# The opening of an adaLN block: c loaded as four rows and turned by one transpose, silu moved ahead, four more unread products

## The chip, the cores and the metric

The kernel runs on one core of a Trainium2 chip. The metric is device time in microseconds (us) of one execution. A core has five engines that run side by side, each through its own instructions in order: TensorE (PE in the profile; its weight loads are PEld), VectorE (DVE), ScalarE (ACT), GpSimd (POOL) and SyncE (SP). SP and ACT also issue transfers (DMAs) between device memory and the on-chip memory; each has a queue for them.

## The reference, cut to what matters

```python
x = A_x                                                   # 1 x 2048 x 512
mod = (_silu(c) @ w_mod).reshape(1, 6, 1, 512)            # c: 1 x 512, w_mod: 512 x 3072
sa, ca, ga, sb, cb, gb = (mod[:, i] for i in range(6))
h = _layernorm(x) * (1 + ca) + sa
x = x + ga * linear_attention(h, A_wqkv, A_wo)            # 32 heads of 16, phi = elu + 1
h = _layernorm(x) * (1 + cb) + sb
x = x + gb * (((h @ B_w_gate) * (h @ B_w_up)) @ B_w_down) # inner width 1376
```

Everything is float32. The first thing that attention needs is h: the normalized rows of x, scaled by 1 + ca and shifted by sa. These two vectors come from c and from columns of w_mod. So the opening of the kernel has two strands that meet: the statistics of the first 512 rows of x, and silu(c) times two column blocks of w_mod.

## The kernel before, in words

**Tiling.** The 2048 rows of x are worked in four chunks of four tiles, 128 rows each. A float32 product is made of three products of rounded halves (high by high, high by low, low by high), so a projection of 128 rows by 512 columns over a depth of 512 is 12 products of 128 x 128 by 128 x 512. The stages follow each other: K, V and Q work with the first normalization; the attention's output; the gated part with its second normalization, as a block product with sums of halves; the product with w_down. The order of the instructions on each engine is the order in which the code calls them: nothing is rescheduled. Most on-chip buffers come from one pool of 99 tiles, and products go to two pools of four PSUM banks.

**The opening** is written out by hand at lines 457 to 538. Its parts, by function and line:

- Transfers (127 to 143): the four x tiles of the first chunk go by turns to SP's and ACT's queue. Then SP takes c as one row of 512 (line 130). Then come halves of two column blocks of w_mod (`load_half`: 256 columns of two k), two on each queue, and the rest on SP. Line 56 says which rows of w_mod a partition holds: `(p k)`, so partition p holds rows 4p to 4p + 3. Transfers are counted by eight completion counters in turn; a transfer waits until the one eight before it, which used the same counter, has landed.
- `keep_on(n)` (152 to 154) issues n products of zeros into a bank that nobody reads.
- `silu_a` (163 to 167) turns c from one row into four columns: a product of each 128-element piece with a single one. ACT then takes exp(-c). `silu_b` (169 to 172) makes silu from it with three small steps on VectorE, into `sc`.
- `Norm.stats` (253, 254), `rstd_of` (262 on VectorE, 265 on POOL) and `nmr_of` (270) give mean and deviation of two tiles at a time. `xhat` (280 on ACT, 277 on VectorE) writes a normalized tile, and `transpose_token` (294) turns its four 128 x 128 pieces on TensorE.
- The scale and shift: `block_pe` (403) multiplies pieces of w_mod with `sc` on TensorE, depth by depth. `half_sum` (179 on ACT, 183 on VectorE) instead sums four scaled rows of w_mod per partition into a tile f; `block_one` (414) then adds f over the partitions with a product by ones. `block_out` (418) writes 128 values of each vector into `both`.
- `mod_h` (425), `mod_f` (432) and `mod_l` (437) apply scale and shift and split the result in halves. `weight_h` (442) and `weight_l` (445) split the weights. `cells` (454) are the products of the first projection (K).

The order on TensorE is thus: 14 unread products; c turned; 1 unread; tile 0 transposed; 2 unread; tile 1 transposed; the scale or shift by `block_pe` of the first 128 columns; 1 unread; tiles 3 and 2 transposed; `block_one`; 2 unread; the sums of the next 128 columns; `cells`.

Of the kernel before, what the change touches and what calls it, by code (L numbers as in the profile page):

```python
# [14 lines left out]
P = 128  # L15
# [7 lines left out]
def tile_adaln_block(  # L23
# [12 lines left out]
    nc = tc.nc  # L36
# [3 lines left out]
    KD = D // P  # L40
    NJ = 4
# [8 lines left out]
    xv = x[0].rearrange("(c p j) d -> c j p d", p=P, j=NJ)  # L50
# [2 lines left out]
    wo_v = wo.rearrange("(k p) n -> k p n", p=P)  # L53
    wg_v = w_gate.rearrange("(k p) f -> p k f", p=P)
    wu_v = w_up.rearrange("(k p) f -> p k f", p=P)
    wm_v = w_mod.rearrange("(p k) n -> p k n", k=KD)

    pool = lambda name, bufs, **kw: ctx.enter_context(tc.tile_pool(name=name, bufs=bufs, **kw))
    consts = pool("consts", 1)
# [10 lines left out]
    def T(p, tag, shape=(P, D), dt=F32, bufs=None):  # L70
        cnt[0] += 1
        return p.tile(list(shape), dt, tag="t" if p is tiles else tag, name=f"{tag}_{cnt[0]}", bufs=bufs)

    def B(tag, shape=(P, D), dt=F32):

        return T(tiles, tag, shape, dt)
# [8 lines left out]
    ident = consts.tile([P, P], F32, name="ident")  # L85
    make_identity(nc, ident)
    ones = consts.tile([P, 1], F32, name="ones")
# [21 lines left out]
    def load(src, tag, by=None):  # L109
        raw = B(tag, (P, *src.shape[1:]))[:src.shape[0]]  # L110
        (by or nc.sync).dma_start(raw, src)
        return raw
# [12 lines left out]
        return [load(wqkv_v[k, :, n * D:(n + 1) * D], "raw") for k in range(KD)]  # L125

    two = (nc.sync, nc.scalar)
    xts = [[load(xv[0, j], "x", two[j % 2]) for j in range(NJ)]]
    c_row = B("f")[:1]
    nc.sync.dma_start(c_row, c)  # L130
    raw_half = {}
    raw_half[1, 0] = load_half(1, 0, two)
    raw_half[0, 0] = load_half(0, 0, two)
# [18 lines left out]
    def keep_on(n):  # L152
        for _ in range(n):
            nc.tensor.matmul(ps_idle, idle[:, :P], idle, start=True, stop=True)  # L154
# [6 lines left out]
    ct = ps_m[:, 4 * KD:5 * KD]  # L161

    def silu_a():
        of_k = c_row.rearrange("o (p k) -> o k p", k=KD)
        for k in range(KD):
            nc.tensor.matmul(ct[:, k:k + 1], of_k[:, k], ones[:1], start=True, stop=True)
        nc.scalar.activation(ce, ct, AF.Exp, scale=-1.0)

    def silu_b():
        nc.vector.tensor_scalar(ce, ce, 1.0, None, op0=ALU.add)  # L170
        nc.vector.reciprocal(ce, ce)
        nc.vector.tensor_mul(sc, ct, ce)
# [212 lines left out]
    n0 = norm[0]  # L385
# [21 lines left out]
    def half_sum(v, half, *ks, on=None):  # L407
        if 0 in ks:
            sums[v, half] = B("f")[:, :D // 2]
        mod_acc(sums[v, half], [raw_half[v, half][k // 2][:, k % 2] for k in range(KD)], ks, on)  # L410
# [29 lines left out]
    def weight_h(k):  # L440
        wk.append((B("w", dt=F32R), B("w", dt=F32R)))
        nc.scalar.activation(wk[k][0], raw_k[k], AF.Copy)
# [11 lines left out]
                nc.tensor.matmul(kps[t], x[:, t * P:(t + 1) * P], w, start=k == 0 and part == 0,  # L454
                                 stop=k == KD - 1 and part == 2)

    keep_on(14)
    n0.stats(0)
    nc.vector.tensor_copy(ones_r, ones.to_broadcast([P, P]))
    n0.stats(1)  # L460
    n0.rstd_of(0, 2)
    n0.stats(2)
    n0.nmr_of(0, 2)
    n0.xhat(0)
    silu_a()
    keep_on(1)
    n0.xhat(1)
    n0.stats(3)
    n0.rstd_of(2, 4)
    n0.transpose_token(0)  # L470
    silu_b()
    half_sum(0, 0, 0, on=nc.scalar)
    n0.nmr_of(2, 4)
    n0.xhat(2)
# [3 lines left out]
    block_pe(1, 0)  # L478
    half_sum(0, 0, 1, 2, 3)
    weight_h(0)  # L480
    keep_on(1)
    n0.transpose_token(3)
    n0.transpose_token(2)
    block_one(0, 0)
# [151 lines left out]
    for i in range(4, NT):  # L636
        ch, j = divmod(i, NJ)
# [910 lines left out]
```

## Time and profile before

| | us |
|---|---|
| median of three timed runs | 561.05 (560.29, 561.05, 563.6) |
| the profiled execution's own time | 556.42 |
| its span, first to last instruction | 554.5 |
| TensorE busy in the span | 547.8 |
| VectorE, ScalarE, GpSimd busy | 420.2, 297.1, 176.9 |

The profile is of one execution. Times in its rows count from the start of the span. A row of the chain of waits has start, length and what ran, followed back from the last instruction; a row of the timeline has start, length, engine, line, operation and tiles (written <- read), shape and count, and in brackets the idle time ahead of it with what ended it; a row of a window table gives, for a stretch, its length, and for each engine its busy time and how many instructions began, then the granted clock of TensorE, the busy share of the transfer engines and the rate in GB/s. Lines of the tables refer to the kernel before.

### The profile page before, as it was taken

Reading aid. Unit: us, or ns where it says so; the run is one execution under the profiler, and the core shown is the slowest. Engines: PE = TensorE matmul, PEld = TensorE weight load, DVE = VectorE, ACT = ScalarE, POOL = GpSimd, SP = SyncE. Lnnn points to the kernel's source line nnn. Section 1 sums busy time; section 2 is a strip of 40 time slices with the busy share of each in tenths; the row PEclk is TensorE's granted clock in tenths of the full one; section 3 lists DMA queues with packets and bytes.
Section 4 is the critical chain, followed back from the end, with each engine's and each line's share of the span. In section 5 each row is a group of like instructions: output and inputs, shape, how many; then the busy total and the mean of one; then the engine's idle time right before and its main releaser. Section 6 shows DMA issues by size and latency. Waiting matters only on the chain.

```text
span 554.5 us, 8037 instructions
## 1 busy us (share of the span) xinstructions
PE 547.8 (99%) x2744; PEld 460.8 (83%) x2744; DVE 420.2 (76%) x755; ACT 297.1 (54%) x528; POOL 176.9 (32%) x183
## 2 busy tenths in 40 slices
PE   8999999999999999999999999999999999999996
PEld 7888888888888888888888888878888888888886
DVE  5868779978998998865655766854567878778696
ACT  4976858456567876654545355442443525443540
POOL 2000000003527645343556644400512524242400
PEclk9999999999999999999999999999999999999999
DMA  8900224203230045195888635499575534442004
GB/s 287 386 11 1 76 77 151 77 1 76 77 115 2 0 155 186 39 316 178 284 285 276 218 123 202 157 373 331 177 262 190 182 122 147 133 139 77 0 1 152
DMA packets 56746, 83.75 MB, mean 151 GB/s; under 512 B 6593, under 2 KB 21697, under 8 KB 56706
## 3 DMA queue, kind: packets, MB, share of 16 engines
q1 hardware_dynamic: 55874, 82.21, 44.2%
q10 hardware_dynamic: 832, 1.05, 0.5%
q8 instruction: 21, 0.34, 0.3%
q14 instruction: 19, 0.16, 0.1%
HBM read 53.54 MB, written 29.69 MB: 150 GB/s over the span
## 4 chain that ended last, share of the span: by engine, by line
PE 99%; DVE 0%; issue 0%; DVEq 0%
PE bank L1039 38%; PE acc L1198 8%; PE acc L853 8%; PE bank L222 5%; PE bank L224 5%; PE bank L223 5%; PE acc L1121 4%; PE acc L1122 4%; PE acc L1123 4%; PE acc L373 3%; PE acc L372 3%; PE acc L371 3%; PE bank L287 2%; PE acc L454 2%; PE acc L154 1%; PE bank L828 1%
## 5 line engine op out<-in xcount | busy, mean ns | idle before, releaser
L1039 PE MATMUL bank<-h,w 128*128 128x512 f32 (+1 forms) x924 | 220.5, 391 | 0.0
L1039 PEld LDWEIGHTS bank<-h,w 128*128 128x128 f32 (+1 forms) x924 | 168.7, 186 | 36.6 <-issue 0.4
L1045 ACT ACTIVATE bank<-bank 128x512 f32<-128x512 f32 (+1 forms) x45 | 26.2, 581 | 131.0 <-PE bank L1039 130.7
L1002 POOL TENSOR_TENSOR w<-raw,w 128x256 fp32r<-128x256 f32 (+3 forms) x22 | 24.2, 1100 | 79.7 <-ACT w L995 64.9
L1222 DVE TENSOR_TENSOR x<-acc,x 128x256 f32<-128x256 f32 x108 | 39.2, 415 | 10.2 <-PE acc L1198 9.6
L1198 PE MATMUL acc<-w,kh 128*128 128x256 f32 x252 | 46.8, 282 | 0.0
L222 PE MATMUL bank<-w,h 128*128 128x512 f32 x112 | 44.1, 394 | 0.0
L1198 PEld LDWEIGHTS acc<-w,kh 128*128 128x128 f32 x252 | 41.4, 190 | 3.1 <-DVE x L1222 0.2
L224 PE MATMUL bank<-w,h 128*128 128x512 f32 x112 | 43.7, 390 | 0.0
L223 PE MATMUL bank<-w,h 128*128 128x512 f32 x112 | 43.7, 390 | 0.0
L853 PE MATMUL acc<-w,xh 128*128 128x512 f32 x128 | 40.7, 399 | 0.0
L1065 DVE TENSOR_TENSOR phi<-bank,g 128x512 f32<-128x512 f32 (+1 forms) x22 | 15.1, 687 | 29.8 <-PE bank L1039 28.4
L702 POOL TENSOR_TENSOR f<-h,zb 128x512 f32<-128x512 f32 x12 | 17.5, 1472 | 62.9 <-ACT zb L682 48.8
L265 POOL TENSOR_TENSOR rstd<-ve,half 128x4 f32<-128x4 f32 (+3 forms) x12 | 10.5, 879 | 82.9 <-DVE ve L262 70.5
L1095 DVE TENSOR_TENSOR g<-bank,u 128x512 f32<-128x512 f32 (+1 forms) x22 | 15.2, 690 | 28.4 <-ACT u L1045 25.0
L1121 PE MATMUL acc<-w,kh 128*128 128x512 f32 (+1 forms) x92 | 35.9, 390 | 0.0
L1122 PE MATMUL acc<-w,kh 128*128 128x512 f32 (+1 forms) x92 | 35.9, 390 | 0.0
L1123 PE MATMUL acc<-w,kl 128*128 128x512 f32 (+1 forms) x92 | 35.8, 389 | 0.0
L1198 PE MATMUL acc<-w,kl 128*128 128x256 f32 x126 | 35.6, 283 | 0.0
L1045 ACT ACTIVATE u<-bank 128x512 f32<-128x512 f32 (+1 forms) x44 | 26.2, 595 | 12.6 <-PE bank L1039 12.4
L1128 DVE TENSOR_TENSOR x<-acc,x 128x512 f32<-128x512 f32 x44 | 28.1, 681 | 5.8 <-PE acc L1123 5.8
L280 ACT ACTIVATE n<-x,nmr,rstd 128x512 f32<-128x512 f32 x31 | 23.7, 807 | 11.2 <-DVE nmr L270 11.0
(198 smaller groups left out, 1189.1 us busy)
## 6 DMA issues: line engine op xcount, KB each, us to landing
right<-w SPq DMA_DIRECT2D x56, 256.0 KB, 3.8
w<-right SPq DMA_DIRECT2D x56, 256.0 KB, 3.6
x<-in_A_x_dram SPq DMA_DIRECT2D x22, 256.0 KB, 5.4
raw<-in_w_mod_dram SPq DMA_DIRECT2D x22, 256.0 KB, 3.5
raw<-in_B_w_down_dram SPq DMA_DIRECT2D x20, 256.0 KB, 3.2
side_s<-h SPq DMA_DIRECT2D x16, 256.0 KB, 2.6
h<-side_s SPq DMA_DIRECT2D x16, 256.0 KB, 5.7
raw<-in_A_wqkv_dram SPq DMA_DIRECT2D x12, 256.0 KB, 5.4
```

Of the source, the lines that this page charges most:

```text
L222: nc.tensor.matmul(ps, ah, bh, start=begin and i == 0, stop=False)
L223: nc.tensor.matmul(ps, ah, bl, start=False, stop=False)
L224: nc.tensor.matmul(ps, al, bh, start=False, stop=end and i == n - 1)
L853: nc.tensor.matmul(yps[i], x, y, start=fresh and k + n == 0, stop=k == KD - 1 and n == 2, skip_group_check=True)
L1039: mm = lambda x, y, **kw: nc.tensor.matmul(ps, x[:, k], y, skip_group_check=True, **kw)
L1045: nc.scalar.activation(out, x, AF.Copy)
L1121: nc.tensor.matmul(dn[j], hh[:n, a:b], dh[:n], start=i == 0, stop=False)
L1122: nc.tensor.matmul(dn[j], hh[:n, a:b], dl[:n], start=False, stop=False)
L1123: nc.tensor.matmul(dn[j], hl[:n, a:b], dh[:n], start=False, stop=i == n_of - 1)
L1128: nc.vector.tensor_tensor(xt, dn[j], xt, op=ALU.add)
L1198: mm = lambda x, y, **kw: nc.tensor.matmul(ps, x[:, a:b], y, skip_group_check=True, **kw)
L1222: nc.vector.tensor_tensor(xt[:, halves[at]], banks[b][:, part], xt[:, halves[at]], op=ALU.add)
```

## The change

The c vector is loaded as four rows of 128, second on ACT's queue between its two x tiles, and one transpose with a 4 x 4 identity turns it into 128 x 4. Since element 128k + p of c now stands in partition p, column k, w_mod is viewed in the same order, `(k p)`, wherever it is loaded. The turn and the exponential (`silu_a`) move ahead of the normalization, behind 13 unread products, with 5 behind them. `silu_b` moves ahead of the statistics of the fourth tile. The normalization of tiles 0 and 1 on ACT is issued together. One more unread product stands behind the sums of `half_sum`, ahead of the transposes of tiles 3 and 2. That is three more unread products around the turn (18 instead of 15) and one more later.

```diff
-    wm_v = w_mod.rearrange("(p k) n -> p k n", k=KD)
+    wm_v = w_mod.rearrange("(k p) n -> p k n", p=P)
...
-    xts = [[load(xv[0, j], "x", two[j % 2]) for j in range(NJ)]]
-    c_row = B("f")[:1]
-    nc.sync.dma_start(c_row, c)
+    xts = [[load(xv[0, j], "x", two[j]) for j in range(2)]]
+    c_k = B("f")[:KD, :P]
+    nc.scalar.dma_start(c_k, c[0].rearrange("(k p) -> k p", p=P))
+    xts[0] += [load(xv[0, 2 + j], "x", two[j]) for j in range(2)]
...
     def silu_a():
-        of_k = c_row.rearrange("o (p k) -> o k p", k=KD)
-        for k in range(KD):
-            nc.tensor.matmul(ct[:, k:k + 1], of_k[:, k], ones[:1], start=True, stop=True)
+        nc.tensor.transpose(ct, c_k, ident[:KD, :KD])
         nc.scalar.activation(ce, ct, AF.Exp, scale=-1.0)
...
-    keep_on(14)
+    keep_on(13)
+    silu_a()
+    keep_on(5)
     n0.stats(0)
...
     n0.nmr_of(0, 2)
-    n0.xhat(0)
-    silu_a()
-    keep_on(1)
-    n0.xhat(1)
+    n0.xhat(0, 1)
+    silu_b()
     n0.stats(3)
     n0.rstd_of(2, 4)
     n0.transpose_token(0)
-    silu_b()
     half_sum(0, 0, 0, on=nc.scalar)
...
     weight_h(0)
-    keep_on(1)
+    keep_on(2)
     n0.transpose_token(3)
```

## The prediction, made before the changed kernel was run

> **What bounds the kernel now.** I read the page first: the span, the busy shares, the granted clock and the chain that ended last.
>
> ```profile
> span 554.5 us, 8037 instructions
> ...
> PE 547.8 (99%) x2744; PEld 460.8 (83%) x2744; DVE 420.2 (76%) x755; ACT 297.1 (54%) x528; POOL 176.9 (32%) x183
> ...
> PEclk9999999999999999999999999999999999999999
> ...
> PE 99%; DVE 0%; issue 0%; DVEq 0%
> ```
>
> TensorE is busy for 547.8 of 554.5 us and carries 99% of the chain, at a granted clock in its top tenth in every slice. So time is saved only by taking work off TensorE, or by starting its useful work earlier; whatever moves the first projection moves the end by the same amount, as long as TensorE then runs on without holes.
>
> The diff touches only the opening, so I went next to the chain of waits of the first 16 us. A row gives start, length, line and count of TensorE's work; L154 is the unread product, L166 the four products that turn c, L294 the transposes of normalized rows, L403 and L414 the scale and shift sums, L454 the first projection of K.
>
> ```profile
> 1.98 5.17 PE acc L154 x14
> 7.15 1.95 PE acc L166 x8
> 9.11 0.43 PE acc L154
> 9.53 0.44 PE bank L294 x4
> 9.97 0.47 PE acc L154 x2
> 10.43 0.44 PE bank L294 x4
> 10.87 0.79 PE acc L403 x8
> 11.66 0.34 PE acc L154
> 12.00 0.87 PE bank L294 x8
> 12.87 0.12 PE acc L414 x2
> 12.99 0.57 PE acc L154 x2
> 13.56 0.79 PE acc L403 x8
> 14.34 0.22 PE acc L414 x2
> 14.56 1.26 PE acc L454 x5
> ```
>
> TensorE has no hole here, but part of this is filling: twenty unread products in all, eight half-passes for c (1.95 us), and only from 14.56 on useful products. To see what really gates that point I took the timeline of the same stretch. (A row: start, length, engine, line, what is written from what; in brackets idle time before it and what ended it.)
>
> ```profile
> 5.07 1.28 ACT L280 ACT_TABLE_LOAD   x1 [5.07 <-DMA x<-in_A_x_dram]
> ...
> 6.85 0.71 POOL L265 TENSOR_TENSOR rstd<-ve,half 128x2 f32<-128x2 f32 x1 [4.13 <-DVE ve L262]
> ...
> 7.59 0.16 DVE L270 SCALAR_TENSOR_TENSOR nmr<-mv,rstd 128x2 f32<-128x2 f32 x1
> 7.67 0.69 DVE L253 BATCH_NORM_STATS2 st<-x 128x6 f32<-128x512 f32 x1
> 7.79 0.81 ACT L280 ACTIVATE n<-x,nmr,rstd 128x512 f32<-128x512 f32 x1 [1.43 <-DVE nmr L270]
> ...
> 8.61 0.17 DVE L262 TENSOR_SCALAR ve<-mv 128x2 f32<-128x2 f32 x1
> ...
> 8.86 0.70 POOL L265 TENSOR_TENSOR rstd<-ve,half 128x2 f32<-128x2 f32 x1 [1.30 <-DVE ve L262]
> ...
> 9.35 0.17 DVE L170 TENSOR_SCALAR ce<-ce 128x4 f32<-128x4 f32 x1 [0.57 <-ACT ce L167]
> ...
> 9.92 0.15 DVE L270 SCALAR_TENSOR_TENSOR nmr<-mv,rstd 128x2 f32<-128x2 f32 x1
> ...
> 10.46 0.80 ACT L280 ACTIVATE n<-x,nmr,rstd 128x512 f32<-128x512 f32 x1
> 10.59 1.53 DVE L183 SCALAR_TENSOR_TENSOR f<-raw,sc,f 128x256 f32<-128x256 f32 x3
> ...
> 12.60 0.30 PEld L414 LDWEIGHTS acc<-ones,f 128*128 128x128 f32 x2
> ...
> 13.03 0.16 DVE L418 TENSOR_TENSOR both<-acc,unit 128x2 f32<-128x2 f32 x1 [0.92 <-PE acc L414]
> ```
>
> Read backwards: the first modulated tile needs `both` (L418, 13.03), which had waited for the sums L414 (TensorE, 12.60). Those need the scale sum f, whose last of three steps on VectorE ends at 10.59 + 1.53 = 12.12. TensorE comes to L414 only at 12.60, so before the change TensorE's own order decides, with VectorE 0.48 us behind it as the next limit. That 0.48 is what this change can win at most here before VectorE takes over, and the change also adds to VectorE's side.
>
> **The change part by part.**
>
> *TensorE.* It loses L166 (1.95 us). It gains one transpose of four rows, and four unread products: 13 + 5 where 14 + 1 stood, and 2 where 1 stood ahead of the later transposes. No row shows a 4x128 transpose; the ends are 0.11 (L294, 0.44 for four) and 0.49 (two of the half-passes of L166, 1.95/8 each). I take 0.11, since it is one instruction of L294's kind, which runs as one pass. The unread ones are 0.47/2 = 0.24 each in the chain. Net 1.95 - 0.11 - 4 x 0.24 = 0.88 us less on TensorE ahead of L454, if it never waited. But it will wait. The first thirteen end near 7.15 - 0.24 = 6.91, c is turned by about 7.1, five more end by 8.3. The first normalized tile is ready at 7.79 + 0.81 = 8.60, unchanged, since its cause (L265 to 7.56, then L270 at 7.59) is ahead of everything moved. So TensorE idles some 0.3 us, and begins L294 at about 8.8 (weights to load after the release), where the chain has 9.53. From there its queue is 0.44 + 0.47 + 0.44 + 0.79 + 0.34 + 0.24 + 0.87 = 3.59 us up to L414: about 12.4, where the chain has 12.87.
>
> *VectorE.* The three small steps that finish silu (L170 to L172) now stand behind L270 and ahead of the fourth tile's statistics (L253 at 7.67). From 9.35 to the next step at 9.92 they take 0.57 us, so statistics, variance (8.61) and POOL's power (8.86) move by 0.57: POOL then ends at 8.86 + 0.70 + 0.57 = 10.13. Before, L270 came at 9.92 because it stood behind silu, although POOL was done at 9.56; now it comes at 10.13 + 0.04 = 10.17, 0.25 later. Behind it on VectorE wait the fourth tile (L277) and the three steps of f: they end at 12.12 + 0.25 = 12.37. For these the move costs; silu is no longer on the way, POOL's second power is.
>
> *ScalarE.* The exponential goes ahead of both first tiles. Its table load (5.07, 1.28 long) ends at 6.35, before c is turned, so the exponential runs at about 7.2 to 7.4 and L280 still starts at 7.79. The second tile no longer waits behind the exponential and follows the first at about 8.6; the next tile (10.46) now waits for L270: 10.17 + 0.15 + 0.04 = 10.36. It ends at 11.16, and the chain needs it near 11.9. All of it is cover for TensorE.
>
> *The join.* L414 starts at the later of 12.37 + 0.04 (VectorE) and about 12.4 (TensorE): 12.4 against 12.60. **That is the whole gain: 0.2 us.** Everything behind it up to L454 (two unread products, eight sums, two more sums: 0.57 + 0.79 + 0.22) is TensorE's own order as before. Ends: if VectorE's move costs nothing, TensorE's order alone gives up to 0.5; if the three steps cost twice their 0.57 there, 12.37 becomes 12.94 and L414 comes 0.4 late. Nearest the rows is 0.2.
>
> *Transfers and queues.*
>
> ```profile
> 1.72 0.33 SPq L130 DMA_DIRECT2D f<-in_c_dram  x1
> 1.73 3.31 ACTq L111 DMA_DIRECT2D raw<-in_w_mod_dram  x2
> ...
> 6.60 1.99 SPq L111 DMA_DIRECT2D raw<-in_w_mod_dram  x4
> ```
>
> The row of c leaves SP's queue (0.33 us of issuing) and goes second on ScalarE's, ahead of the fourth x tile and of its first w_mod load: those issue 0.33 later, SP's w_mod loads 0.33 earlier. ScalarE's queue ends at 5.04 all the same, since its last load waits for the first x tile. c now lands behind one x tile instead of two; before, its products began at 7.08 to 7.15 without a wait for it, so 6.9 is safe unless the four short rows are slow. By the completion counters, SP's second batch of w_mod loads (6.60) waited first for the third x tile and now for c, so one load may go out some 1.5 us sooner.
>
> ```profile
> 8.00:9.00 1.00, 1.00 (x5) 1.00 (x5) 0.71 (x3) 0.60 (x1) 0.14 (x1) 1.00 1.08 391
> ...
> raw<-in_w_mod_dram ACTq DMA_DIRECT2D x2, 256.0 KB, 6.0
> ```
>
> The transfers fill their engines at that time (share 1.08, 391 GB/s), so an earlier place in a queue brings nothing and could delay another by one 256 KB load, some 0.67 us at that rate. The load at risk is ScalarE's second: its issue ends at 5.04 and it lands 6.0 us from issue, before 11.0. f's second step ran at about 11.1 (10.59 and a third of 1.53) and will run at 11.35, so a delay of 0.67 could reach past it by 0.3. I cost this at 0, with +0.3 as the end. The new order of w_mod's rows leaves the size of each piece unchanged (four rows per partition become one of each quarter) and I cost it at 0; no wait for a w_mod load stands in the rows above.
>
> **Sum:** -0.2 us (-0.5 to +0.5). The profiled execution took 556.42 us in all; by the sum 556.2. The median of the three timed runs is 561.05 (560.29 to 563.6), 4.63 above the profiled one, which no row here explains. Against that median: 560.85.
>
> **The clock, as row and rule.** The first products show a slow start:
>
> ```profile
> 2.00:4.60 2.60, 2.60 (x6) 2.14 (x7) 1.00 0.92 264
> 4.60:7.20 2.60, 2.55 (x9) 1.66 (x8) 1.00 0.96 312
> ```
>
> Six start in 2.6 us, 0.43 each; in the next 2.6 us nine start although the last part stands at L166. The clock column shows 1.00 in both, so the pace is the evidence: TensorE warms up near 4.6 us. The Trainium skill, "TensorE: Matmul & The Clock Gate", Part 1, says that the clock gate opens after about 3.4 us of sustained work, falls back to half after an idle window, and that its window runs freely, so the point varies between executions; Part 4 says that transposes do not count as busy in the same way. The trace agrees on the pace and cannot show the variation. By that rule the thin stretch from 7.15 to 14.56 might lose the clock in one execution and not in another, in either kernel; the sum would be as above when it does not, and the two clock rivals when it does.
>
> **The rivals.**
>
> 1. *The fuller opening keeps a clock that the timed runs lose.* For it: the timed runs stand 4.63 above the profiled one, and half a clock over 4.6 to 14.56 would cost up to (14.56 - 4.6)/2 = 5.0, nearly that gap. The change takes out the 1.95 us of one-row products and adds 0.94 us of full ones. Against: the profiled run of before shows no loss there, and the gap may lie outside the opening. If true, 1.7 to 4.6 less: about 557.5.
>
> 2. *The other side: the clock falls in the new hole, or c comes late.* The hole is at about 8.3 to 8.8, behind the fifth unread product. If the clock halves for the rest of the thin stretch, 8.8 to 14.56, it costs up to 2.9 us: 563.9. It decides only if 0.3 to 0.5 us of idleness suffices. Against: before, TensorE went through 1.95 us with one active row and kept its pace at 9.97 (two in 0.47). Likewise c: each 1 us that it lands after 7.4 delays the exponential, both first tiles behind it, and all else by 1 us; it had landed by 7.15 behind two tiles.
>
> 3. *Nothing gained, or a little lost:* silu ahead of the statistics costs VectorE more than 0.48 and takes TensorE's place as the limit. From a delay of 0.48 on L414 it decides; at twice the price, +0.4: 561.4. For it: 0.25 of the 0.48 are gone by my own count.
>
> **How the numbers follow.** Forecast (-0.5 to +0.1): 0.63. Rival 1: 0.17. Rival 2: 0.10. Rival 3: 0.10. A measurement tells no less than about 1% (5.6 us) from no change. The forecast and rival 3 are within it; rival 1 passes it only beyond its upper end, if timed runs had lost more than 5 us (0.06 of its 0.17); rival 2 only with a clock lost for longer than the opening (0.05 of 0.10). So faster 0.06, same 0.89, slower 0.05. The range goes from the middle of rival 1 to rival 2 and takes in the runs' own spread: 557.0 to 563.6.
>
> **What would show it.** In the changed profile: one short transpose writing from f near 6.9 instead of L166; the exponential near 7.2, ahead of the first normalized tile at 7.79; the second tile near 8.6; L270's second at 10.2 (VectorE's price, right if between 10.1 and 10.3); the first transposes at 8.8; `both` first written near 12.8; the first projection 0.2 earlier. A pace of 0.43 anywhere after 5 us shows rival 2; `both` waiting on sums that wait for f, later than 13.03, shows rival 3. A time below 558 with the opening only 0.2 shorter means that the timed runs' own loss has gone, rival 1. The prediction is wrong if the end moves by more than the opening does.

## The result and the profile after

The changed kernel takes 555.53 us in the median (555.22 to 556.06, 13 runs), the kernel before, run beside it, 560.6 us (556.28 to 563.6, 13 runs). The ratio is 0.9909, with a 95% interval of 0.988 to 0.9939. That is 5 us less, where the prediction had 0.2, and it lies below its range. The spread is as telling as the median: 7.3 us before, 0.8 us after. Even the shortest of the 13 runs of before, 556.28, is longer than the longest after, 556.06.

The two profiled executions show little of this: 556.42 us against 555.36. First the page of the changed kernel, then its chain of waits in the opening (start, length, line and count; L279 is the first normalized tile on ScalarE, L155 is now the unread product, L293 the transposes of rows, L402 and L413 the sums, L453 the first projection).

```profile
span 553.5 us, 8031 instructions
...
PE 547.2 (99%) x2741; PEld 459.6 (83%) x2741; DVE 419.8 (76%) x755; ACT 297.1 (54%) x528; POOL 176.9 (32%) x183
...
PEclk9999999999999999999999999999999999999999
```

```profile
7.70 0.82 ACT n L279
8.52 0.04 issue
8.57 0.65 PE bank L293 x4
9.22 0.47 PE acc L155 x2
9.69 0.44 PE bank L293 x4
10.13 0.79 PE acc L402 x8
10.92 0.57 PE acc L155 x2
11.48 0.87 PE bank L293 x8
12.36 0.31 PE acc L413 x2
12.66 0.57 PE acc L155 x2
13.23 0.79 PE acc L402 x8
14.02 0.22 PE acc L413 x2
14.24 1.26 PE acc L453 x5
```

The first projection comes at 14.24 instead of 14.56, 0.32 earlier, and TensorE runs on from there as before. The opening does what the sum said, give or take 0.1. At the last step on VectorE, behind the last product, the lead is still 0.39 us (the kernel before, then the changed one):

```profile
549.92 0.42 DVE x L1222
```

```profile
549.53 0.42 DVE x L1220
```

From this step to the end of the span it takes 4.6 us before (549.92 to 554.5) and 4.0 after (549.53 to 553.5): some 0.6 to 0.7 us of the change lie in the last stores, where the prediction had nothing. The traces of all six kernels here that load c as four rows have the shorter end, all eight traces with c as one row the longer one; why, no run shows. Of the 5 us the two executions thus show about 1. The other 4 are in executions that this pair does not show, so the first experiment was to look at more executions of the kernel before.

### The profile page after: what moved, and what is told of

Its sections match the earlier page's. It is cut to its first block, busy times and chain, and to the rows that moved or that the text cites. A ratio compares the mean times of both kernels' runs of the same rounds, so it can differ in the third digit from the quotient of the medians.

```text
span 553.5 us, 8031 instructions
## 1 busy us (share of the span) xinstructions
PE 547.2 (99%) x2741; PEld 459.6 (83%) x2741; DVE 419.8 (76%) x755; ACT 297.1 (54%) x528; POOL 176.9 (32%) x183
## 4 chain that ended last, share of the span: by engine, by line
PE 98%; DMA 1%; DVE 0%; ACT 0%; POOL 0%; issue 0%; DVEq 0%; POOLq 0%
PE bank L1037 38%; PE acc L1196 8%; PE acc L851 8%; PE bank L221 5%; PE bank L223 5%; PE bank L222 5%; PE acc L1120 4%; PE acc L1119 4%; PE acc L1121 4%; PE acc L372 3%; PE acc L370 3%; PE acc L371 3%; PE bank L286 2%; PE acc L453 2%; PE bank L826 1%; PE acc L776 1%
## 5 line engine op out<-in xcount | busy, mean ns | idle before, releaser
L1043 ACT ACTIVATE u<-bank 128x512 f32<-128x512 f32 (+1 forms) x44 | 26.2, 595 | 12.6 <-PE bank L1037 12.4
L1000 POOL TENSOR_TENSOR w<-t,w 128x512 fp32r<-128x512 f32 (+1 forms) x22 | 29.7, 1348 | 0.0
```

What stands on the lines that cost most here:

```text
L1000: sub = lambda out, x, y: (on or nc.gpsimd).tensor_tensor(out, x, f32(y), op=ALU.subtract)
L1043: nc.scalar.activation(out, x, AF.Copy)
```

## The experiments

Each run is set against runs of the kernel before on the same chip side by side. In the expectations, theory A is the loss of TensorE's clock; B and C are the loads, of c and of w_mod; A2, D and E are narrower forms of A.

### The kernel before, looked at again (b_again, b_look2, b_look3)

No edit.

> The kernel before, unchanged, to see the clock and the span of each of its executions. Theory A (the clock): the long executions lose TensorE's clock in the opening; they should show a lower mean granted clock or a slow pace (0.43 us per product) behind 5 us, with spans that spread from 554 to 562. Theory B (transfers: c's one row and w_mod's row order come late in most executions): the same spread, but with a full clock and a hole on TensorE ahead of the turn of c or the scale sums.

> The kernel before, one more profiled execution, to see where the clock falls. Theories D and E: wherever the execution is longer than 557, a fall of the granted clock for windows of some 3.4 us in the stretch from 7 to 20 us, with the lost time equal to half of what runs at half clock.

> As b_look2, one more execution: lost time equal to half of the time at half clock, in the opening.

Twelve runs: median 560.92 (557.99 to 564.47), ratio 1.0022 (0.9982 to 1.0063). They fall in groups, and each group has its own mean granted clock:

```
time, us             mean granted clock   runs of 12
557.99 to 558.06     0.996                2
560.15 to 561.36     0.992                5
563.25 to 564.47     0.986 to 0.987       5
```

A mean that lies 0.008 below 1 over 558 us stands for 4.5 us lost, 0.014 below over 562 us for 7.9. Taken off, every group comes to about 556. The two further looks fell next to the first group and in the last one: 558.22 and 563.58. So the spread of the kernel before is the clock. (A mean of 0.997 to 0.999 need not mean a loss in the opening. The execution of the prediction has 0.998, and its clock falls only behind the last product: 1.00 from 545.00 to 549.92, 0.68 behind.) Where the clock falls is shown by stretches of these executions. (A row: the stretch, its length, then for each engine the busy time and instructions begun, the granted clock, the share of the transfer engines, GB/s.) First b_again, then b_look2, then b_look3, and last the first execution, which the prediction was made from.

```profile
6.91:10.32 3.41, 3.41 (x18) 2.91 (x16) 2.23 (x8) 1.40 (x3) 1.41 (x2) 1.00 1.07 374
10.32:17.15 6.83, 6.83 (x30) 6.25 (x28) 2.85 (x8) 2.91 (x6) 0.00 (x0) 0.50 1.07 375
17.15:20.56 3.41, 3.41 (x21) 2.81 (x21) 2.57 (x8) 3.28 (x7) 0.00 (x0) 1.00 1.04 386
```

```profile
6.02:9.44 3.42, 3.42 (x15) 2.91 (x14) 2.71 (x9) 1.43 (x4) 1.13 (x2) 1.00 1.06 371
9.44:12.85 3.41, 3.41 (x15) 2.96 (x15) 2.51 (x8) 2.90 (x6) 0.29 (x1) 0.50 1.09 357
12.85:16.26 3.41, 3.41 (x29) 3.25 (x29) 1.17 (x3) 1.23 (x2) 0.00 (x0) 1.00 1.05 381
```

```profile
7.62:11.04 3.42, 3.42 (x17) 2.90 (x16) 1.74 (x10) 1.77 (x4) 0.70 (x1) 1.00 1.07 371
11.04:24.69 13.65, 13.65 (x50) 11.95 (x49) 7.81 (x17) 7.42 (x13) 0.00 (x0) 0.50 1.06 383
```

```profile
5.63:9.04 3.41, 3.41 (x16) 2.86 (x14) 2.91 (x10) 1.54 (x2) 0.89 (x2) 1.00 1.00 343
9.04:12.46 3.42, 3.42 (x27) 3.15 (x27) 2.51 (x8) 3.01 (x6) 0.52 (x1) 1.00 1.08 356
```

The record of the granted clock starts at 6.91, 6.02, 7.62 and 5.63 us, and each set of rows with it. Until then products run at half pace, 0.43 us each by the prediction's rows, and the column shows 1.00 for want of a record; at this point the clock opens. In the first three executions it is taken back one window of 3.41 us later, for two windows, one and four: 6.83, 3.41 and 13.65 us at 0.50. Half of these are 3.4, 1.7 and 6.8 us lost. Added to the 556.42 of the execution that lost none, they give 559.8, 558.1 and 563.3, close to the three groups. In the fourth, the execution of the prediction, it was not taken back before the last product. In these four executions more windows are lost the later the clock opens: none, one, two and four at 5.63, 6.02, 6.91 and 7.62. The Trainium skill, "TensorE: Matmul & The Clock Gate", Part 1, gives a window of 3413 ns that runs freely; the lengths here agree with it. In the profile TensorE counts as busy all through the windows ahead of the loss (3.41 of 3.41, 3.42 of 3.42), so no idle window was needed, and busy time does not show the cause. In b_again the chain of waits does:

```profile
7.74 1.95 PE acc L166 x8
9.69 0.43 PE acc L154
10.12 0.54 PE bank L294 x4
10.66 0.85 PE acc L154 x2
11.51 0.85 PE bank L294 x4
12.37 1.50 PE acc L403 x8
13.87 0.64 PE acc L154
14.50 1.71 PE bank L294 x8
```

The window 6.91 to 10.32 holds the whole of L166: four products, which stand in the profile as eight instructions of one row and one column each, here called half-passes. Behind 10.32 everything takes double: two unread products 0.85 instead of 0.47, the eight sums 1.50 instead of 0.79, the eight transposes 1.71 instead of 0.87.

### More unread products in the kernel before (b_18, b_mix)

```diff
-    keep_on(14)          # b_18
+    keep_on(18)
...
             nc.tensor.matmul(ct[:, k:k + 1], of_k[:, k], ones[:1], ...)
+            keep_on(1)   # b_mix
```

> The kernel before with 18 unread products ahead of the turn of c instead of 14, nothing else. It puts 4 x 0.23 = 0.9 us more on TensorE's path ahead of everything. Theory A: the longer dense stretch opens the clock in every execution: 556.5 to 558, spread under 1.5 us. Theory B: 0.9 us longer than the kernel before with the same spread, about 561.5.

> The kernel before with one more unread product behind each of the four products that turn c; everything else as before. As many as in b_18 (four), but inside the thin stretch. Theory A2: the clock stays, at the price of 4 x 0.23 on TensorE's path: 557.0, spread under 2 us. Theory C: about 561.5 with the spread of before.

b_18: 557.92 (556.99 to 564.86), ratio 0.9976 (0.9934 to 1.0019); three of twelve runs at a mean clock of 0.996 or less, against 23 of 29 of the kernel before beside it. b_mix: 558.68 (557.79 to 563.91), ratio 0.9993 (0.9956 to 1.003); five of twelve, against 29 of 35. So four more unread products, in front or in between, keep the clock in more executions but cost time in all: the shortest run of b_18 is 1.0 us longer than the shortest of the kernel before beside it (556.99 against 555.97), that of b_mix 1.8 (557.79 against 556.03), twice the 0.9 expected. Neither is the 5 us.

### The changed kernel with the old number of unread products (a_15)

```diff
     silu_a()
-    keep_on(5)
+    keep_on(2)
...
-    keep_on(2)
+    keep_on(1)
     n0.transpose_token(3)
```

> The changed kernel with the unread products taken back to the old count: 13 + 2 around the turn of c and 1 behind the scale sums. Theory A: the spread of the kernel before comes back, median 558 to 562. Theory B: no change from 555.5, since c, w_mod's order and the moved silu are all kept.

556.01 (555.61 to 556.15, six runs), ratio 0.99 (0.9855 to 0.9945), no mean clock under 0.999. Theory A was wrong on this point: the gain does not need the added products.

### c's load, w_mod's order and the transpose alone (b_c4)

```diff
-    wm_v = w_mod.rearrange("(p k) n -> p k n", k=KD)
+    wm_v = w_mod.rearrange("(k p) n -> p k n", p=P)
...
-        of_k = c_row.rearrange("o (p k) -> o k p", k=KD)
-        for k in range(KD):
-            nc.tensor.matmul(ct[:, k:k + 1], of_k[:, k], ones[:1], start=True, stop=True)
+        nc.tensor.transpose(ct, c_k, ident[:KD, :KD])
```

The loads of c and x are those of the changed kernel; silu and the unread products stay where they were.

> The kernel before with c as four rows on the other queue, one transpose and w_mod's new row order, but with the old places of silu and the old unread products (14, 1, 2, 1, 2). Theory A: TensorE gets the 1.95 us free but fills them with waiting, so the clock is lost at least as often: spread stays, median 559 to 563. Theory B: most of the gain is here, 555.5 to 557 with a small spread.

555.39 (555.16 to 559.52), ratio 0.9893 (0.9862 to 0.9924); one of twelve runs lost the clock (559.52 at 0.993). This is the whole gain, as theory B had it and theory A had not. But b_again had shown the clock falling, so the question became which of the three edits keeps it.

### w_mod's order alone, and products instead of the transpose (b_kp, b_c4_prod)

```diff
-        of_k = c_row.rearrange("o (p k) -> o k p", k=KD)      # b_kp, with w_mod as (k p)
+        of_k = c_row.rearrange("o (k p) -> o k p", p=P)
...
-        nc.tensor.transpose(ct, c_k, ident[:KD, :KD])         # b_c4_prod, from b_c4
+        for k in range(KD):
+            nc.tensor.matmul(ct[:, k:k + 1], c_k, ident[:KD, k:k + 1], start=True, stop=True)
```

> The kernel before with w_mod's new row order alone (c read in the matching order from its one row, still four products). Theory A2 (the eight one-row half-passes leave TensorE so thinly used for 1.95 us that its clock is taken back for two windows in many executions): nothing changes, 558 to 563 in the median, spread 8 us, mean clocks down to 0.986. Theory C (the loads of w_mod in the old order, or c's late row, hold something up): 555.5, no spread.

> As b_c4 (c as four rows on ScalarE's queue, w_mod's new order, old places and unread products), but c is turned by four products with columns of the identity instead of one transpose: again eight half-passes of some 0.23 us each. Theory A2: the spread of the kernel before comes back, median 558 to 563. Theory C: 555.5 as b_c4, since the loads are the same.

b_kp: 556.4 (555.86 to 557.13), ratio 0.9932 (0.99 to 0.9964). b_c4_prod: 555.86 (555.29 to 556.66), ratio 0.9918 (0.9881 to 0.9954). No mean clock in either is under 0.997. Both still have eight half-passes, and both keep the clock: theory A2, in the form that these half-passes lose it by being there, is wrong too. Theory C came near both numbers (0.9 us over its 555.5 in b_kp, 0.4 in b_c4_prod), but it does not explain the fallen clock of b_again. In the profiled execution of b_kp the clock opens at 7.26, later than in b_again, and is kept:

```profile
7.26:10.67 3.41, 3.41 (x25) 2.81 (x23) 2.78 (x12) 2.55 (x5) 1.08 (x2) 1.00 1.09 369
10.67:14.08 3.41, 3.41 (x29) 3.25 (x30) 2.30 (x6) 2.36 (x5) 0.00 (x0) 1.00 1.07 368
```

The instructions of line 166 show what else the new order changes. First the kernel before, then b_kp. (Minimum, median and maximum of one, in ns; first and last start in us.)

```profile
L166 PEld LDWEIGHTS acc<-ones,f x8: 305/325/325, 7.1 to 8.7; 1*128 1x128 f32 x8
L166 PE MATMUL acc<-ones,f x8: 367/367/390, 7.1 to 8.7; 1*128 1x1 f32 x8
```

```profile
L166 PEld LDWEIGHTS acc<-ones,f x8: 181/187/187, 7.8 to 8.6; 1*128 1x128 f32 x8
L166 PE MATMUL acc<-ones,f x8: 245/245/266, 7.8 to 8.6; 1*128 1x1 f32 x8
```

With `(p k)` the weights of one product are every fourth element of c; with `(k p)` they lie next to each other. A weight load of step four takes 325 ns, one of unit step 187 (187 also in b_c4_prod, where the expectation had taken the eight for as slow as before). The eight take 1.95 us in the chain of the kernel before and 0.98 in that of b_kp:

```profile
7.90 0.98 PE acc L166 x8
8.87 0.43 PE acc L154
```

So three theories remained: the loads (C), the length of the thin stretch (D), or the step itself (E).

### Length against step and loads (b_kp_twice, a_ones, a_step4)

```diff
+            nc.tensor.matmul(ps_m[:, 5 * KD + k:5 * KD + k + 1], of_k[:, k], ones[:1], ...)  # b_kp_twice
             nc.tensor.matmul(ct[:, k:k + 1], of_k[:, k], ones[:1], start=True, stop=True)
...
     silu_a()
-    keep_on(5)                                                # a_ones, from the changed kernel
+    for k in range(KD):
+        nc.tensor.matmul(ps_m[:, 5 * KD + k:5 * KD + k + 1], c_k[:1], ones[:1], ...)
...
+    x_k = xts[0][0][:1].rearrange("o (p k) -> o k p", k=KD)   # a_step4: x_k[:, k] instead of c_k[:1]
```

The columns that the added products write are not read.

> As b_kp (c read with unit step), but each of the four products is issued twice, once into an unread column: sixteen half-passes of 0.12 us, 1.95 us in all, as long as the eight of before. Theory D (the length of the thin stretch decides): the clock is lost again in many executions, median 558 to 564, spread 8 us. Theory E (the step of four elements in the weight load itself decides): 556.4 to 557.4, no spread, mean clocks over 0.996.

> The changed kernel with the five unread products behind the turn of c replaced by four unread products of one row with a single one: the eight half-passes of before, 1.95 us, which end near 8.8 (0.2 us behind the first normalized tile). Theory A2: the clock is lost in many executions: median over 557, up to 564, mean clocks under 0.995. Theory C: 555.7, no spread.

> The changed kernel with the five unread products behind the turn of c replaced by four unread products of a row of x, read with a step of four elements, with a single one: eight half-passes as slow as those of before (0.23 each, 1.95 us in all). a_ones had the same number with unit step, 1.0 us in all. Theories D and E both: clock lost in many executions, median over 558, up to 564. If neither holds (it needs the kernel before's order around it): 556.7 as a_ones.

b_kp_twice: 559.26 (555.92 to 563.93), ratio 1.0007 (0.9963 to 1.0051); ten of twelve runs at a mean clock of 0.996 or less. The weights are read with unit step, the stretch is long again (7.86 to 9.73, 1.87 us), and the loss is back as it was in the kernel before. b_kp_twice has b_kp's loads of c and w_mod, which b_kp runs without loss, so theory C falls here as well. Its profiled execution shows the same picture as b_again, one window and then two at half:

```profile
7.16:10.57 3.41, 3.41 (x25) 2.90 (x25) 1.84 (x10) 1.62 (x3) 1.06 (x2) 1.00 1.09 369
10.57:17.40 6.83, 6.83 (x30) 6.15 (x29) 3.14 (x9) 3.10 (x7) 0.00 (x0) 0.50 1.06 377
```

That decides for D against C, and against E as far as E needs the step of four. The expectation of a_ones took its stretch for 1.95 us; with unit step it is 1.03:

```profile
8.45 1.03 PE acc L459 x8
9.48 0.02 issue
```

Its result is 556.72 (555.5 to 558.68), ratio 0.9937 (0.9902 to 0.9972), one of twelve runs at 0.993. a_step4, where the same number is read with step four, takes 557.57 (556.41 to 563.26), ratio 0.9989 (0.9948 to 1.003), with five of twelve at 0.993 or less. Its profiled execution lost four windows, behind a stretch of 1.99 us:

```profile
8.40 1.99 PE acc L460 x8
```

```profile
8.20:11.61 3.41, 3.21 (x18) 3.09 (x18) 1.46 (x6) 2.02 (x4) 0.00 (x0) 1.00 1.09 366
11.61:25.26 13.65, 13.65 (x49) 11.90 (x48) 7.97 (x19) 7.12 (x12) 0.70 (x1) 0.50 1.06 384
```

So inside the changed kernel, too, a one-row stretch of 2 us brings the loss back, and one of 1 us does so in one run of twelve. Step and length change together between a_ones and a_step4; what separates them is b_kp_twice.

## Why the prediction was wrong, point by point

**The step that failed** is the one from the profiled execution to the median: "the median of the three timed runs is 561.05, 4.63 above the profiled one, which no row here explains", followed by -0.2 against that median. The profiled execution was one of the few in which the clock held (6 of 29 and 6 of 35 in two later sets of runs). Its profile could price the opening, but most of the executions behind the median had lost 1.7 to 6.8 us more, to windows at a clock of 0.50. The gap of 4.63 was most of the effect to be predicted, and the forecast carried it over unchanged. Its own sign of being wrong came true: the end moved by 5 us, the opening by 0.3.

**Rival 1** had the mechanism and nearly the size (1.7 to 4.6 less; the result is 5 less, about 4 of it the clock), with a chance of 0.17. Under the head of a fuller opening it named two parts of the change, the one-row products taken out and the full ones added, and did not say which counts. a_15 shows that the gain stays without the added products, b_18 and b_mix that the added products alone do not bring it. What brings it is the shorter turn of c: by one transpose (b_c4), or already by reading c with unit step (b_kp). Its counter-argument, that the profile of before shows no loss, was an argument from one execution.

**The new order of w_mod's rows** was costed at 0, from the size of the pieces that are loaded. For the transfers that holds in the traces of the kernel before and b_kp: the early w_mod loads land 5.1 us after issue in the median on SP's queue and 6.0 on ScalarE's in both. The prediction missed that the same edit sets how c is read into TensorE's weights: eight half-passes at 0.24 us become eight at 0.12 if they are kept, as in b_kp.

**The sum for the opening** was right but small: -0.2 predicted, -0.32 measured between the two profiled executions. Its working sets two unlike points against each other: 12.4 is TensorE's place in the chain, where the kernel before has 12.87, but 12.60 is the start of the weight load. In the chain's terms TensorE's order gave 0.48, so the 0.2 rested on VectorE alone. VectorE's second L270 (now L269) came at 9.98 instead of the expected 10.17, because the three silu steps cost 0.49 in the new place (7.58 to 8.07), not 0.57, and the first x tile landed 0.09 earlier:

```profile
4.56 0.69 DVE L252 BATCH_NORM_STATS2 st<-x 128x6 f32<-128x512 f32 x1 [2.64 <-DMA x<-in_A_x_dram]
...
6.71 0.22 PE L165 MATMUL acc<-ident,f 4*128 4x4 f32 x1
...
7.58 0.16 DVE L169 TENSOR_SCALAR ce<-ce 128x4 f32<-128x4 f32 x1
...
8.07 0.68 DVE L252 BATCH_NORM_STATS2 st<-x 128x6 f32<-128x512 f32 x1
...
9.98 0.16 DVE L269 SCALAR_TENSOR_TENSOR nmr<-mv,rstd 128x2 f32<-128x2 f32 x1 [0.81 <-POOL rstd L264]
...
12.70 0.16 DVE L417 TENSOR_TENSOR both<-acc,unit 128x2 f32<-128x2 f32 x1 [0.54 <-PE acc L413]
```

The transpose of c started at 6.71 (expected near 6.9), and `both` came at 12.70 (expected near 12.8). The join at L413 was as drawn: TensorE and VectorE arrive within 0.2 us of each other. The -0.32 belongs to this pair: before, the fourteen unread products end as the clock opens early or late (7.15 here, 7.74 in b_again), while the chain after runs over x and its first normalized tile (L279) up to 8.52.

**Rival 2** (the clock falls in the new hole) did not occur in the 13 runs. In b_c4, with a wait of 0.54 us on TensorE in the same place and none of the moves, one run of twelve lost the clock; where in that run, no trace shows. **Rival 3** did not occur. **The clock's opening** was put near 4.6 us from the pace of the first products; it is at 5.63 in that execution.

**What stays open.** Whether the added products guard against the one loss in twelve of b_c4 cannot be told from 13 runs without one. Whether pure waiting of 1.95 us would cost the same as the thin products was not tried, and why the last stores end 0.6 to 0.7 us sooner with c as four rows is open. No version tried is shown to beat the changed kernel: b_c4's median is 0.14 lower, but with one run at 559.52.

## What to carry to other kernels

When the timed runs spread far more than the kernel's work can, and the profiled execution stands at their short end, look for the cause of the spread first: list time and mean granted clock run by run before pricing any edit. A TensorE row that reads as busy may be too thin to hold the clock; in an opening, look for the longest stretch of one-row products, and shorten it before padding it. A rearrangement of an operand's layout also sets the step with which weights are read, so it must be priced on TensorE as well as on the transfers.

## What the runs showed of the hardware that was not expected

- A weight load of one row of 128 float32 values takes 325 ns with a step of four elements and 187 with unit step.
- One window of 3.41 us is enough to lose the clock although TensorE reads as busy in all of it. By an estimate from the chains, full products (the unread ones) and the part of an x tile's transposes that falls in it fill 1.52 us of the first window in the kernel before where the clock held (7.15 - 5.63), and 1.46 in b_again where it fell (7.74 - 6.91, 0.43, and 0.20 of the transposes). Counted in the same way, b_kp_twice fell at 1.54 (its window of 3.41 less 1.87). So the limit seems to lie near 1.5 of 3.41, but this count does not divide the executions cleanly. It is a reading of a few of them, not a test.
- Once lost in this opening, the clock stayed at half for one, two or four windows: the price was 1.7, 3.4 or 6.8 us for an opening of 14 us. That it stays away because the thin stretch then lasts longer is likely but not shown.
- Behind the last product, the end of the kernel was 0.6 to 0.7 us shorter in every trace in which c was loaded as four rows on ScalarE's queue. No run shows the cause.
